# Half products of 64 rows beside attention's scores, in place of MLP and projection phases of their own

## The chip, the core and the metric

The kernel runs on one core of one Trainium2 chip. The metric is the device time of one execution in microseconds. Before the change it is 1593.18 us, the median of three runs (1592.98 to 1594.01).

## What is computed

One transformer block over 2,048 rows of 512 features, in fp32: layer norm, attention with 32 heads of 16 features over all rows, residual; then layer norm, an MLP with 1,792 hidden features, residual.

```python
qkv = (layernorm(x) @ wqkv).reshape(B, S, 3, 32, 16)
p = softmax(einsum("bhqd,bhkd->bhqk", q, k) * 16 ** -0.5)
h = x + einsum("bhqk,bhkd->bhqd", p, v).reshape(B, S, 512) @ wo
out = h + silu(layernorm(h) @ w1) @ w2
```

## The kernel before

**Number formats.** Projections and MLP are taken as three half-precision products each: a factor is split into a high and a low part of fp16, and high x high, low x high and high x low are summed. A "product" of one 128x512 tile of Q or K is 3 x 4 = 12 matmuls (`project_qk`, L590); a tile of the MLP's first layer is also 12; a tile of 128 output rows of its second layer is 3 x 14 = 42. Each of these matmuls contracts over 128 rows.

**Attention** is cut into 32 items: four blocks of 512 queries times eight sets of four heads. An item has 16 groups of 128 keys, 512 groups in all. A group (`scores`, L462; `values`, L856) is:
- four scores, one for each head: a matmul of 64 rows (48 rows of split Q and K and some with the row maximum, so that the product comes out with the maximum taken off), into a bank of PSUM; two heads of an item lie in rows 0 to 63 of TensorE's array, two in rows 64 to 127;
- an exponential on ScalarE for each score, from PSUM into a tile `pt`;
- four values, one for each head: `pt` as the moving fp32 operand, 17 columns of V and a column of ones as the stationary one, accumulated over the item's groups in the bank `pv`. They run two groups behind the scores (`LAG = 2`).

**Maxima.** The softmax's row maximum must be known before an item's scores. For each item 64 matmuls of 48 rows give Q K again, and VectorE reduces each bank to a maximum (`maximum`, L285: L301 reduces one bank, L299 two at once). A maximum of one row half stands beside a score of the other half. There are 2,048 of them, and they must be done one item ahead:

```python
            mm(space[:, n + m, :], qs[i % RING][64 * h:64 * h + 48, a, qt * P:qt * P + P],
               ks[i % RING][64 * h:64 * h + 48, a, kb * 512:kb * 512 + 512], start=True, stop=True)
        ...
            pin(nc.vector.tensor_reduce(of[:, j:j + 1], space[:, n, :], axis=AX.X, op=ALU.max))
```

A planner (`maxima`, L1324) says in each group how many maxima are issued, at most three. Finished maxima are turned and written into the rows of Q through DRAM or from PSUM (`place_far`, L338, `place_max`, L351).

**Order.** Every engine's queue follows the program text (`keep_in_program_order`), so the order is written out by hand. `soon` and `tick` delay steps by whole groups. The sequence is:
1. The projections of V and of the first set of Q and K, with maxima in pairs of banks (`burst`, L438) beside them.
2. 24 late projections, Q and K of the other three sets for four blocks, each with six maxima in pairs; the first two groups' scores stand between the last ones.
3. Attention, in which Q and K of coming items are loaded into a ring of five (`RING`).
4. In items 8, 16 and 24 (`FIRSTS`) the output projection of the block before (`output`, L1184), and after each of them that block's MLP (`finish_block`, L1204, `mlp`, L1118) with attention standing still: 14 first products with Silu, then the second layer in four accumulators, with 138, 138 and 110 maxima (`BESIDE`) in pairs between. The scores of the next two groups stand at its end.
5. After the last item the output projection and MLP of the last block (`finish_last`, L1221).

**PSUM** has eight banks of 128x512 fp32 (`space`). In attention scores take turns in four of them (`st`), maxima in three (`sm`), and one is `pv`:

```python
    attention_banks = 4, 5, last_bank, idle_bank
    lay_out(st=range(4), sm=attention_banks[:3])
    pv = space[:, idle_bank, :]
```

**Weights** of the MLP are split early in attention (`split_weights`, L1003, from group 12 on, one tile in four groups), stored to DRAM and read back tile by tile (`load_weights`, L989) into a ring of eight: w1 once and w2 twice for each block.

Of the kernel before, what the change touches and what calls it, by code (L numbers as in the profile page):

```python
# [43 lines left out]
SPLIT = 12  # L44
# [4 lines left out]
PTS = 16  # L49

EARLY = 8

RING = 5
# [12 lines left out]
JOINT = 2  # L66
AHEAD = 4
# [4 lines left out]
BESIDE = (138, 138, 110)  # L72
OUTPUT = 8

# [10 lines left out]
SPAN_2 = 12 * (FC - 2) - 3  # L85

MORE = 2, 2, 0
# [3 lines left out]
def attention_mlp_kernel(ctx: ExitStack, tc: tile.TileContext, x, wqkv, wo, w1, w2, out):  # L91
# [5 lines left out]
    def mm(*a, **k):  # L97
        tc.keep_in_program_order(nc.tensor.matmul(*a, **k))  # L98
# [12 lines left out]
    def act(fn, *a, **k):  # L111
        pin(getattr(nc.scalar, fn)(*a, **k))  # L112
# [80 lines left out]
    factors = const.tile([P, 14], F32, name="factors")  # L193
    sigma, inverse = factors[:, :4], factors[:, 4:8]
    w1_s, w2_s, wo_s, o_s = (sigma[:, n:n + 1] for n in range(4))
    h_f, g_s, out_f, wo_f, o_minus, o_twice = (factors[:, n:n + 1] for n in range(8, 14))
# [141 lines left out]
    def place_far(piece):  # L338

        i, _ = piece  # L340
        mt = small.tile([P, 32], F16, name="mt")
        dve("transpose", mt, split.pop(piece))
        issue = dma_beside if at["beside"] else dma
# [27 lines left out]
    at = {"item": 0, "done": 0, "half": 0, "step": 0, "due": 0, "attention": False, "group": None, "ready": 0, "next": 0, "blocks": True, "beside": False}  # L371
# [20 lines left out]

    def found_maxima(piece):
        g = at["group"]
        marked = g is not None and g + 1 in marks
        if g is None or marked or piece[1] is None and start_of(piece) - g > FAR:
            soon(WAIT + 1 if g is None or marked else CALM, place_far, piece)
            finish_max(piece, marked)
            return
        late.setdefault(at["step"] + WAIT, []).append(piece)  # L400
        unfinished.append(piece)
        found_at["step"] = at["step"]

    def one_max(half=None, n=None):
# [7 lines left out]
        if at["blocks"]:  # L412

            i = min(range(2), key=lambda n: (todo[n, half] or todo[n, 1 - half] or [(n, KC)])[0][1])
# [6 lines left out]
    def two_max(n):  # L421

        i = next_item()
        if i == ITEMS:
            return
        both = [next(((t[1], m, t) for t in todo[m, 0] if (*t[:4], 1) in todo[m, 1]), None)
                for m in (range(2) if at["blocks"] else (i,))]
        both = min((x for x in both if x), default=None)
# [26 lines left out]
    pts, den, pools = {}, {}, []  # L455
    taken = iter(range(10 ** 6))

    def pt_tile(name, dtype=F32):
        pool_of = pools[next(taken) % PTS >= EARLY]
        return pool_of.tile([P, 512], dtype, tag="pt", name=name)  # L460

    def scores(g, k, kind="st"):  # L462
# [7 lines left out]
        pts[g, k] = pt_tile("pt")  # L470
        act("activation", pts[g, k], ps, AF.Exp, scale=qk_f)


    with ExitStack() as pa:
        pb = pa.enter_context(ExitStack())
        lay_out(sm=range(5), st=range(5, 8))
        wp = pa.enter_context(tc.tile_pool(name="wp", bufs=1))
        wvp = pb.enter_context(tc.tile_pool(name="wvp", bufs=1, side="right"))
        xp = pa.enter_context(tc.tile_pool(name="xp", bufs=3))
        wqk_h = wp.tile([P, DC, 2 * D], F16, name="wqk_h")  # L480
        wqk_l = wp.tile([P, DC, 2 * D], F16, name="wqk_l")
        wv_h = wp.tile([P, DC, D], F16, name="wv_h")
        wv_l = wp.tile([P, DC, D], F16, name="wv_l")
        xth = [wp.tile([P, DC, 512], F16, name=f"xth{b}") for b in range(NB)]
        xtl = [wp.tile([P, DC, 512], F16, name=f"xtl{b}") for b in range(NB)]

        wqk0_h, wqk0_l = (wvp.tile([P, DC, 2 * P], F32R, name=name) for name in ("wqk0_h", "wqk0_l"))
        wv0_h, wv0_l, xth0, xtl0 = (wvp.tile([P, DC, 512], F32R, name=name) for name in ("wv0_h", "wv0_l", "xt0_h", "xt0_l"))

        xts = [ks[2 + b % 2].rearrange("p a n -> p (a n)").bitcast(F32).rearrange("p (t d) -> p t d", d=D)  # L490
               for b in range(NB)]

        scaled = ks[RING - 1].rearrange("p a n -> p (a n)").bitcast(F32).rearrange("p (t n) -> p t n", n=512)
        scaled, staged = ([scaled[:, t, :] for t in half] for half in ((0, 1), (2, 3)))
        flat = va.rearrange("p c h d -> p (c h d)")
        raw_v, *raw_qk = (flat[:, -n * DC * D:][:, :DC * D].rearrange("p (c n) -> p c n", c=DC) for n in (3, 2, 1))

        def load_x(b, parts=1):
            n = 4 // parts
            for t in range(0, 4, n):  # L500
                r0 = b * 512 + t * P
                dma(xts[b][:, t:t + n, :], x[r0:r0 + n * P, :].rearrange("(t p) d -> p t d", p=P))

        sq = small.tile([P, 3], F32, name="sq", bufs=1)

        free = qs[RING - 1].rearrange("p a n -> p (a n)").bitcast(F32)
        rest_sq, norms = free[:, :sum(PIECES)], free[:, 64:68]
        pieces = [w.rearrange("(p r) f -> p (r f)", p=P)[:, 512 * n:512 * (n + 1)]
                  for w, count in zip((w1, w2, wo), PIECES) for n in range(count)]

        def square_into(out, src, n):
            act("activation", out, src, AF.Square, accum_out=rest_sq[:, n:n + 1])

        def square_rest(u):

            n = u - 7
            if 0 <= n < len(pieces):
                square_into(staged[n % 2], staged[n % 2], n)
            n = u - 5
            if 0 <= n < len(pieces):  # L520
                dma_beside(staged[n % 2], pieces[n])

        def measure_rest():
            n = sum(PIECES)
            ps = bank("sm")
            mm(ps[:, :n], ones, rest_sq, start=True, stop=True)
            dve("tensor_reduce", norms[:, :2], ps[:, :28].rearrange("p (a k) -> p a k", a=2), axis=AX.X, op=ALU.add)
            dve("tensor_reduce", norms[:, 2:3], ps[:, 28:n], axis=AX.X, op=ALU.add)
            pool("tensor_scalar", norms, norms, 1e-30, None, op0=ALU.add)
            pool("tensor_tensor", norms, norms, expos, ALU.pow)  # L530

        def set_factors():
            dve("tensor_scalar", sigma[:, :3], norms[:, :3], TOP, None, op0=ALU.mult)
            dve("tensor_scalar", sigma[:, 3:], norms[:, 3:], TOP / BOUND, None, op0=ALU.mult)
            dve("tensor_scalar", sigma.bitcast(U32), sigma.bitcast(U32), 0x7F800000, None, op0=ALU.bitwise_and)
            dve("reciprocal", inverse, sigma)
            for to, a, f in ((h_f, inverse[:, :1], 1 / LN), (g_s, w1_s, 1 / 32.0), (o_minus, o_s, -1.0),
                             (o_twice, o_s, 2.0), (out_f, inverse[:, :1], 32.0)):
                pool("tensor_scalar", to, a, f, None, op0=ALU.mult)
            pool("tensor_tensor", out_f, out_f, inverse[:, 1:2], ALU.mult)  # L540
            pool("tensor_tensor", wo_f, inverse[:, 2:3], inverse[:, 3:], ALU.mult)

        def square(n, raw):
            act("activation", ks[RING - 1].rearrange("p a n -> p (a n)").bitcast(F32).rearrange(
                "p (c n) -> p c n", c=DC), raw, AF.Square, accum_out=sq[:, n:n + 1])

        def split_scaled(high, rest, raw, scale, engine="dve"):
            act("mul", high, raw, scale)
            if engine == "pool":
                pool("tensor_scalar", raw, raw, scale, 1.0, op0=ALU.mult, op1=ALU.mult)  # L550
                low(rest, raw, high, engine)
            else:
                dve("scalar_tensor_tensor", rest, raw, scale, high, op0=ALU.mult, op1=ALU.subtract)

        def split_qk(n, engine="dve"):
            g, key = divmod(n, 2)
            cols = slice(key * D + g * P, key * D + (g + 1) * P)
            split_scaled(wqk_h[:, :, cols], wqk_l[:, :, cols], raw_qk[key][:, :, g * P:(g + 1) * P], qk_w, engine)

        def split_first(key):  # L560
            cols, raw = slice(key * P, (key + 1) * P), raw_qk[key][:, :, :P]
            act("copy", wqk0_h[:, :, cols], raw)
# [887 lines left out]
```

## Time and profile before

| | |
|---|---|
| median of the runs | 1593.18 us |
| span of the profiled execution, first to last instruction | 1591.2 us |
| TensorE, VectorE, ScalarE, GpSimd busy | 99%, 87%, 76%, 30% of the span |
| late projections, 6th to 24th | 110.0 to 178.7 us |
| MLPs of blocks 0, 1 and 2 | 93.1, 93.0 and 87.6 us |
| after the last exponentials | 91.7 us |

The profile gives the span of its execution and no other time of it; the runs' median is 2.0 us longer than that span, and what lies around the span is taken as these 2.0 us. In the profile's rows PE is TensorE, DVE VectorE, ACT ScalarE, POOL GpSimd and SP SyncE, whose queue issues most DMAs. A row of the timeline has start and duration in us, engine, line, operation, and what is written from what; L98, L105, L112 and L115 are lines of helpers, so instructions are told apart by their tiles: `ps<-qs,ks` is a score, `ps<-ks,qs` a maximum's matmul, `ps<-pt,va` a value, `pt<-ps` an exponential, `mx<-ps` a reduce.

### The profile page before, as it was taken

How to read it: one execution, taken by the hardware profiler on the slowest of the kernel's cores; microseconds unless marked ns; L12 is line 12 of the kernel's file. 1: busy time of each engine (PE TensorE's matmuls, PEld its weight loads, DVE VectorE, ACT ScalarE, POOL GpSimd, SP SyncE). 2: the span in 40 equal slices, each digit the busy share in tenths (PEclk: the TensorE clock that was granted, in tenths of full speed). 3: DMA queues.
4: the chain of work that ended last, by engine and by line, in shares of the span. 5: the costliest groups of instructions: out<-in, count | busy, mean ns of one | idle time of the engine just before them, and what ended most of it. 6: DMA issues, size and time to landing. Idle time of an engine off the chain costs nothing. (4 is left out here: it accounts for less than half of the span.)

```text
span 1591.2 us, 28420 instructions
## 1 busy us (share of the span) xinstructions
PE 1579.5 (99%) x10476; PEld 471.7 (30%) x10476; DVE 1386.9 (87%) x2045; ACT 1205.0 (76%) x2384; POOL 484.8 (30%) x764
## 2 busy tenths in 40 slices
PE   9999999999999999999999999999999999999999
PEld 6434222222223322222224322222224322222254
DVE  7999999999998889999988889999986889998432
ACT  6545799999964179999973179999974189999732
POOL 5643544544446101211146101211146101211200
PEclk9999999999999999999999999999999999999999
DMA  6667533443443511121243521112143511100232
GB/s 216 174 177 221 136 86 91 113 119 86 116 100 102 157 47 35 38 51 44 50 102 101 152 53 34 39 41 53 48 104 108 159 40 37 34 12 22 74 87 73
DMA packets 124099, 140.29 MB, mean 88 GB/s; under 512 B 41808, under 2 KB 78736, under 8 KB 123960
## 3 DMA queue, kind: packets, MB, share of 16 engines
q1 hardware_dynamic: 117744, 128.34, 30.5%
q10 hardware_dynamic: 6216, 10.15, 2.3%
q8 instruction: 82, 1.34, 0.4%
q14 instruction: 57, 0.47, 0.1%
HBM read 104.68 MB, written 24.85 MB: 81 GB/s over the span
## 5 line engine op out<-in xcount | busy, mean ns | idle before, releaser
L112 ACT ACTIVATE pt<-ps 128x512 f32<-128x512 f32 x2048 | 1009.3, 611 | 154.4 <-PE ps L98 154.0
L301 DVE TENSOR_REDUCE mx<-ps 128x1 f32<-128x512 f32 x1470 | 925.1, 684 | 48.2 <-PE ps L98 20.3
L98 PE MATMUL ps<-pt,va 128*17 128x512 f32 x4096 | 537.5, 598 | 1.1
L98 PE MATMUL ps<-qs,ks 64*128 64x512 f16 x2048 | 530.9, 379 | 1.5 <-DMA qs<-mn 0.4
L98 PE MATMUL ps<-ks,qs 48*128 48x512 f16 x2048 | 495.4, 380 | 2.6 <-ACT pvs L112 1.1
L299 DVE TENSOR_REDUCE mx<-ps 128x2 f32<-128x1024 f32 x289 | 334.9, 1219 | 43.8 <-PE ps L98 42.5
L98 PEld LDWEIGHTS <-ks 64*128 64x128 f16 x2048 | 149.3, 95 | 549.2 <-issue 432.5
L105 POOL TENSOR_TENSOR ri<-rc,minus 128x16 f32<-128x16 f32 x31 | 90.7, 2926 | 242.5 <-DMA rc<-dn 192.3
L98 PE MATMUL ps<-w,gh 128*128 128x512 f16 (+1 forms) x678 | 154.4, 378 | 0.0
L98 PE MATMUL ps<-hts,w 128*128 128x512 f16 (+1 forms) x708 | 153.3, 369 | 0.0
L98 PEld LDWEIGHTS <-qs 48*128 48x128 f16 x2048 | 126.1, 94 | 77.5 <-issue 61.3
L98 PEld LDWEIGHTS ps<-pt,va 128*17 128x17 f32 x4096 | 69.0, 95 | 225.7 <-issue 205.4
L112 ACT ACTIVATE g<-ps,factors 128x512 f32<-128x512 f32 x56 | 38.4, 686 | 125.0 <-PE ps L98 95.7
L105 POOL TENSOR_TENSOR mx<-mx 128x32 f32<-128x32 f32 x52 | 12.6, 241 | 386.4 <-DVE mx L301 379.8
L98 PEld LDWEIGHTS <-w 128*128 128x128 f16 x708 | 66.5, 98 | 78.6 <-issue 10.2
L98 PEld LDWEIGHTS <-gh 128*128 128x128 f16 x678 | 63.1, 98 | 82.9 <-issue 13.7
L112 ACT ACTIVATE ks<-ps 128x512 f32<-128x512 f32 x30 | 17.9, 598 | 50.5 <-PE ps L98 45.1
L115 DVE SCALAR_TENSOR_TENSOR gh<-g,factors,gh 128x512 f16<-128x512 f32 x14 | 10.5, 751 | 52.1 <-ACT gh L112 52.1
L105 POOL TENSOR_TENSOR sl<-ks,sh 128x512 f16<-128x512 f32 x30 | 34.7, 1157 | 51.5 <-ACT sh L112 38.1
L105 POOL TENSOR_TENSOR gh<-g,gh 128x512 f16<-128x512 f32 x42 | 48.6, 1156 | 3.5
L105 POOL TENSOR_TENSOR ot<-ot,den 128x512 f32<-128x512 f32 (+1 forms) x16 | 20.4, 1273 | 84.4 <-DMA den<-dr 75.8
L98 PE MATMUL ps<-xth,wqk_h 128*128 128x512 f16 x120 | 45.8, 381 | 0.0
(155 smaller groups left out, 919.7 us busy)
## 6 DMA issues: line engine op xcount, KB each, us to landing
w<-w2d SPq DMA_DIRECT2D x98, 256.0 KB
ks<-kd SPq DMA_DIRECT2D x120, 192.0 KB
w<-w1d SPq DMA_DIRECT2D x56, 256.0 KB
ks<-in_B_w_dram ACTq DMA_DIRECT2D x28, 256.0 KB
w<-in_B_w_dram SPq DMA_DIRECT2D x28, 256.0 KB
qs<-qd SPq DMA_DIRECT2D x128, 48.0 KB
kd<-sh SPq DMA_DIRECT2D x16, 256.0 KB
qd<-sh SPq DMA_DIRECT2D x16, 256.0 KB
```

Of the source, the lines that this page charges most:

```text
L98: tc.keep_in_program_order(nc.tensor.matmul(*a, **k))
L105: tc.keep_in_program_order(getattr(nc.gpsimd, op)(*a, **k))
L112: pin(getattr(nc.scalar, fn)(*a, **k))
L115: pin(getattr(nc.vector, fn)(*a, **k))
L299: pin(nc.vector.tensor_reduce(of, space[:, n:n + 2, :], axis=AX.X, op=ALU.max))
L301: pin(nc.vector.tensor_reduce(of[:, j:j + 1], space[:, n, :], axis=AX.X, op=ALU.max))
```

## The change

The work of the late projections from the sixth on and of the MLPs of blocks 0 to 2 is put into attention's groups. A matmul over 128 rows becomes two over 64 rows: `half_product` gives rows 0 to 63 of it in an even group and rows 64 to 127 in the following odd one, both accumulated in one bank, number 3. For that the groups are taken in twos: in such a group the four scores are all of one row half, two of the group and two of its neighbour, and the half products stand in the other row half. `beside_products` lays the steps out: one list for the half products' side, one for the scores' side, maxima put where the lists are shorter.

- 5 late projections stay before attention, with six maxima in pairs each. 19 follow as "chains" of 12 products: five at six half products a group (four groups each), 14 at four (six groups each), so in groups 0 to 103.
- An MLP is 14 chains of 12 and four chains of 42 products at six half products a group, 112 groups after each output item. All results of the first layer are kept (`gates`), w2 is read four times, and Silu is computed as z/2 (1 + tanh(z/2)), with the tanh on ScalarE and the rest on GpSimd.
- In these 440 groups scores have three banks in place of four; maxima keep three; the planner gives four maxima, three where a finished maximum is being placed, and one more where it lags behind (`LEAD`). In the 72 other groups its most is four.
- A group's first half product waits for the last exponential of the group before (`fence`), so that half products of the two row halves don't write the bank at once. At the end of a chain the bank is scaled into SBUF by ScalarE ahead of the last exponential.
- Values run one group behind in these groups. The ring of items has four places. Squares of the weights for their scales, 14 of them, move into attention's first groups. Pool and tile memory is laid out anew.

The diff, cut to its core:

```diff
+SPLIT = 34
+SPACING = 3
-PTS = 16
+PTS = 12
-RING = 5
+RING = 4
-AHEAD = 4
+AHEAD = 6
-BESIDE = (138, 138, 110)
+LEAD = 9
+SWAP = 112
-BURSTS_1 = ({f: 6 for f in range(FC) if f not in (6, 13)},) * 2 + ({f: 6 for f in range(FC) if f % 3 != 1},)
-BURSTS_2 = 12, 12, 10
...
+    def after(ins, earlier):
+        tc.add_manual_dep(ins.ins, earlier.ins.name, mybir.DependencyInfo(
+            mybir.DependencyClass.Sync, mybir.DependencyReason.DATA), reason="row halves in one bank")
...
-        for g in range(1, NG // 2):
-            for m, (b, key) in enumerate([(b, 1) for b in range(NB)] + [(b, 0) for b in range(NB)]):
+    for m, (b, key) in enumerate([(b, 1) for b in range(NB)] + [(0, 0)]):
+        tick()
...
+        project_qk(b, 2 + key, {BESIDE_A1[m]: 6} if m < len(BESIDE_A1) else BESIDE_A, True)
...
-        elif i in FIRSTS:
+        elif i > FIRSTS[0]:
             act("copy", pvs, pv)
...
+    def end_first(f, ps):
+        z = zp.tile([P, 512], F32, name="g")
+        act("mul", z, ps, h_f)
+        def bend():
+            t = zp.tile([P, 512], F32, name="t", tag="oh")
+            act("activation", t, z, AF.Tanh, scale=0.5)
+            pool("tensor_scalar", t, t, 1.0, g_half, op0=ALU.add, op1=ALU.mult)
+            pool("tensor_tensor", t, t, z, ALU.mult)
+            pool("tensor_copy", gates[:, f, 0], t)
+            low(gates[:, f, 1], t, gates[:, f, 0], "pool")
+        soon(2, bend)
...
+    def begin_mlp(b):
+        chains.extend((3 * DC, 6, first_of(f), lambda ps, f=f: end_first(f, ps)) for f in range(FC))
+        chains.extend((3 * FC, 6, second_of(t), lambda ps, t=t: end_second(b, t, ps)) for t in range(4))
+
+    def half_product(j):
+        if j == 0:
+            current["open"].append(next(current["of"]))
+        lhs, rhs = current["open"][current["half"][j] - current["gone"]]
...
+        r = slice(64 * j, 64 * j + 64)
+        ins = mm(space[:, 3, :], lhs[r], rhs[r], start=current["half"] == [0, 0],
+                 stop=current["half"][1] == current["count"] - 1)
+        if "fence" in current:
+            after(ins, current.pop("fence"))
+        current["half"][j] += 1
+
+    def beside_products(g, n):
...
+        side = g % 2
+        heads = [(x, k) for x in (g - side, g - side + 1) for k in range(4) if head(x, k)[1] != side]
...
+        count = current["count"] - current["half"][0] if side == 0 else current["half"][0] - current["half"][1]
+        count = min(current["share"], count)
+        for _ in range(min(n, sum(left))):
+            j = 1 - side
+            if 4 + found[j] > count + found[side] or found[j] == left[j]:
+                j = side
+            if found[j] == left[j]:
+                j = 1 - j
+            found[j] += 1
+        other = [("max", 1 - side)] * found[1 - side]
+        other = [step for m, of in enumerate(heads) for step in [("score", of), *other[m:m + 1]]]
+        same = [("max", side)] * found[side] + [("half", side)] * count
+        short = len(same) - len(other)
+        if short > 0:
+            other[-1:-1] = [("none", 0)] * short
+        waiting = []
+        for m in range(max(len(other), len(same))):
+            for kind, x in same[m:m + 1] + other[m:m + 1]:
+                if kind == "score":
+                    waiting.append(scores(*x))
+                    if len(waiting) < 4:
+                        waiting[-1]()
+                elif kind == "max":
+                    one_max(x)
+                elif kind == "half":
+                    half_product(x)
+        if current["half"][1] == current["count"]:
+            current["end"](space[:, 3, :])
+            current.clear()
+            waiting[3]()
+        else:
+            current["fence"] = waiting[3]()
...
+    first_qk = [(b, 5) for b in range(NB)] + [(0, 4)]
+    other_qk = [(b, 7) for b in range(NB)] + [(0, 6)] + [(b, n) for n in (2, 4, 6) for b in range(1, NB)]
+    chains.extend((3 * DC, share, rows_of_qk(b, n), lambda ps, b=b, n=n: end_qk(b, n, ps))
+                  for units, share in ((first_qk, 6), (other_qk, 4)) for b, n in units)
+    until = 4 * len(first_qk) + 6 * len(other_qk)
+    beside = {*range(until), *(g for m in marks for g in range(m, m + 4 * FC + 4 * FC))}
...
     def maxima(g):
+        ready = at["ready"] = min(ITEMS, i + RING - 1) * 64
+        most = 3 if at["step"] in late else 4
+        if g in beside:
+            at["due"] = 0
+            most += 64 + 4 * (g + LEAD) > at["done"]
+            return max(0, min(most, ready - at["done"]))
...
-        most = 2 if at["step"] in late or c == JOINT and i and i - 1 not in FIRSTS else 3
...
         if g in marks:
-            finish_block(i // 8 - 1, (g - 2, g - 1))
+            begin_mlp(i // 8 - 1)
+            lay_out(st=range(3))
+        elif g - 1 in beside and g not in beside:
+            lay_out(st=range(4))
...
-        if g - LAG >= 0 and not (g in marks or g - 1 in marks):
-            values(g - LAG)
+        while done <= g - (1 if g in beside else LAG):
+            values(done)
+            done += 1
```

Here `scores` returns a function that issues the exponential, so that the last one of a group can be issued behind the chain's end.

More of the change, by code (lines that the diff above doesn't have):

```diff
@@ L342, in place_far @@
         dve("transpose", mt, split.pop(piece))
-        issue = dma_beside if at["beside"] else dma
+        issue = dma
         for b in range(4):
@@ L370, in attention_mlp_kernel @@
     END = 64 * ITEMS
-    at = {"item": 0, "done": 0, "half": 0, "step": 0, "due": 0, "attention": False, "group": None, "ready": 0, "next": 0, "blocks": True, "beside": False}
+    at = {"item": 0, "done": 0, "half": 0, "step": 0, "due": 0, "attention": False, "group": None, "ready": 0, "next": 0, "blocks": True, "loaded": 1}
     agenda, late = {}, {}
@@ new lines, in split_values, with project_v @@
+    def split_values(n):
+        half = slice(2 * n, 2 * n + 2)
+        act("mul", wv_h[:, half], raw_v[:, half], v_w)
+        if n:
+            low(wv_l[:, 2], scaled[1], wv_h[:, 2], "pool")
+        else:
+            low(wv_l[:, 3], scaled[0], wv_h[:, 3], "pool")
+            dve("scalar_tensor_tensor", wv_l[:, half], raw_v[:, half], v_w, wv_h[:, half],
+                op0=ALU.mult, op1=ALU.subtract)
+    def project_v(b, t):
+        ps = bank()
+        weave(product(ps, lambda c: xth[b][:, c, t * P:(t + 1) * P], lambda c: xtl[b][:, c, t * P:(t + 1) * P],
+                      lambda c: wv_h[:, c, :], lambda c: wv_l[:, c, :], DC),
+              {k: (lambda n=n: burst(n)) for k, n in BESIDE_V1.get((b, t), {}).items()})
+        act("mul", va[:, 4 * b + t, :, 0:DH], ps.rearrange("p (h d) -> p h d", d=DH), v_f)
@@ new lines, in turn_x, with columns @@
+    def turn_x(b, t):
+        turn(xts[b][:, t, :], xth[b][:, :, t * P:(t + 1) * P], xtl[b][:, :, t * P:(t + 1) * P],
+             "sm" if b == 1 else "st")
+    load_x(0, parts=4)
+    for dc in range(DC):
+        dma(raw_v[:, dc, :], wqkv[dc * P:(dc + 1) * P, 2 * D:])
+    for key in (1, 0):
+        for dc in range(DC):
+            dma(raw_qk[key][:, dc, :], wqkv[dc * P:(dc + 1) * P, key * D:(key + 1) * D])
+    load_x(1, parts=4)
+    def columns(t):
+        return slice(t * P, (t + 1) * P)
@@ new lines, in idle, with turn_high @@
+    def idle(n):
+        ps = bank()
+        for c in range(n):
+            tr(ps[:, columns(c % 4)], ident, ident)
+    def turn_high(b, t):
+        ps = bank("sm").rearrange("p (c n) -> p c n", n=P)
+        high = xth[b] if b else xth0
+        for c in range(4):
+            tr(ps[:, c, :], xts[b][:, t, c * P:(c + 1) * P], ident)
+        act("copy", high[:, :, columns(t)], ps)
+        return ps
+    idle(20)
+    found = [statistics(xts[0][:, t, :], LN) for t in range(2)]
+    turned, ps_vs = [], []
@@ new lines, in first_rows, with first_products @@
+    def first_rows(t):
+        normalize(xts[0][:, t, :], xts[0][:, t, :], *found[t])
+        turned.append(turn_high(0, t))
+    def first_products(t, *chunks):
+        if t == len(ps_vs):
+            ps_vs.append(bank("st" if t < 3 else "sm"))
+        for c in chunks:
+            mm(ps_vs[t], xth0[:, c, columns(t)], wv0_h[:, c, :], start=c == 0, stop=False)
+    first_rows(0)
+    idle(4)
+    found.append(statistics(xts[0][:, 2, :], LN))
+    act("copy", wv0_h[:, 0, :], raw_v[:, 0, :])
@@ L1051, in split_normal @@
     def split_normal(t):
-        rows, halves[t] = hx.pop(t), parts_of(gp.tile([P, 512], F32, name="g"))
+        rows, halves[t] = hx.pop(t), parts_of(zp.tile([P, 512], F32, name="g"))
         act("copy", halves[t][:, 0], rows)
@@ L1202, in output @@
             found[n] = statistics(rows_of(b, n), LN)
-    def finish_block(b, pending):
-        act("activation", small.tile([P, 1], F32, name="sw"), ident[:, :1], AF.Silu)
-        load_weights("w1", 4)
-        for g in pending:
-            values(g)
-        mlp(b)
     O = ot[(NB - 1) % 2]
```

864 lines of the change are left out of this document (407 added, 457 removed).

## The prediction

> **What bounds the kernel now.** I read the page's engine shares and slices first, then one table of windows cut at the stages, then the timeline of single groups.
>
> ```profile
> PE 1579.5 (99%) x10476; PEld 471.7 (30%) x10476; DVE 1386.9 (87%) x2045; ACT 1205.0 (76%) x2384; POOL 484.8 (30%) x764
> ACT  6545799999964179999973179999974189999732
> ```
>
> TensorE shows 99%, but a busy TensorE is not one at its peak, so this alone says little. ScalarE says what the change is about: it is full in attention and nearly empty three times between, in the MLPs.
>
> ```profile
> 110.00:178.70 68.70, 68.70 (x356) 27.00 (x354) 68.03 (x74) 36.32 (x75) 28.55 (x40) 1.00 0.63 190
> 178.70:427.30 248.60, 247.80 (x1883) 55.24 (x1883) 236.96 (x385) 248.17 (x506) 123.54 (x185) 1.00 0.41 108
> 427.30:472.10 44.80, 44.48 (x295) 11.58 (x295) 41.31 (x70) 34.46 (x70) 16.68 (x24) 1.00 0.41 87
> 472.10:565.20 93.10, 92.38 (x476) 35.84 (x468) 82.46 (x79) 23.69 (x35) 35.94 (x59) 1.00 0.44 123
> 786.60:831.80 45.20, 44.68 (x295) 11.59 (x295) 41.37 (x70) 34.52 (x71) 16.70 (x24) 1.00 0.34 76
> 831.80:924.80 93.00, 92.35 (x476) 35.83 (x468) 82.69 (x79) 23.63 (x34) 34.48 (x53) 1.00 0.44 123
> 1146.30:1189.50 43.20, 43.00 (x289) 11.53 (x289) 37.73 (x64) 34.53 (x71) 16.70 (x24) 1.00 0.36 79
> 1189.50:1277.10 87.60, 87.24 (x448) 34.36 (x440) 66.31 (x63) 23.58 (x34) 33.84 (x50) 1.00 0.44 130
> 1499.50:1591.20 91.70, 88.15 (x466) 44.09 (x456) 27.74 (x48) 24.61 (x38) 3.17 (x8) 1.00 0.25 69
> ```
>
> Columns: stretch, length, then busy time of PE, weight loads, DVE, ACT, POOL, granted clock, DMA share, GB/s. The rows are the 19 late projections (68.7 us), attention up to the first output item, each output item with its MLP, and the tail. In the MLPs ACT is busy 24 of 93 us, but DVE 82 of 93, because the maxima go on there in pairs. So the idle engine is ACT alone; DVE and TensorE have little left to fill. The clock is 1.00 throughout.
>
> Now one attention group on TensorE:
>
> ```profile
> 255.42 0.39 PE L98 MATMUL ps<-qs,ks 64*128 64x512 f16 x1
> 255.42 0.60 PE L98 MATMUL ps<-ks,qs 48*128 48x512 f16 x2
> 255.65 0.59 PE L98 MATMUL ps<-qs,ks 64*128 64x512 f16 x2
> 255.87 0.38 PE L98 MATMUL ps<-ks,qs 48*128 48x512 f16 x1
> 256.08 0.38 PE L98 MATMUL ps<-qs,ks 64*128 64x512 f16 x1
> 256.39 1.05 PE L98 MATMUL ps<-pt,va 128*17 128x512 f32 x8
> 257.38 0.39 PE L98 MATMUL ps<-qs,ks 64*128 64x512 f16 x1
> ```
>
> A score of one row half and a maximum of the other start together; such a step takes (256.08 - 255.42) / 3 = 0.22 us. From the last step to the values is 0.31, from there to the next group 0.99. A group is 3 x 0.22 + 0.31 + 0.99 = 1.96 us with three maxima. Its fixed part is 1.30.
>
> ```profile
> 243.66 0.60 PE L98 MATMUL ps<-ks,qs 48*128 48x512 f16 x2
> 244.12 1.89 DVE L301 TENSOR_REDUCE mx<-ps 128x1 f32<-128x512 f32 x3 [0.30 <-PE ps L98]
> L301 DVE TENSOR_REDUCE mx<-ps x290: 679/681/693, 235.5 to 429.9; 128x1 f32<-128x512 f32 x145
> 1345.26 0.69 DVE pvs L115
> 1345.95 0.04 issue
> 1345.99 60.91 PE ps L98 x464
> 564.80 0.61 PE L98 MATMUL ps<-qs,ks 64*128 64x512 f16 x4
> 565.22 2.06 ACT L112 ACTIVATE pt<-ps 128x512 f32<-128x512 f32 x4 [40.56 <-PE ps L98]
> L112 ACT ACTIVATE pt<-ps x395: 591/603/646, 235.7 to 429.8; 128x512 f32<-128x512 f32 x198
> ```
>
> DVE waits for nothing else when its reduce starts 244.12 - 243.66 = 0.46 after the maximum's matmul; a reduce takes 0.68 and they follow at (1.89 - 0.68) / 2 = 0.60. TensorE starts 0.04 after the DVE ends (the chain of waits, last three rows of it). So a bank of a maximum is free again 0.46 + 0.68 + 0.04 = 1.18 us after its matmul started. An exponential starts 0.42 after its score, follows the one before at (2.06 - 0.60) / 3 = 0.48, and takes 0.60. Three maxima use 1.80 of 1.96 on DVE, four exponentials 1.92 on ACT: all three engines are near balance in attention, with TensorE the longest.
>
> **The change, part by part.** Durations are of the profiled execution; the median is 1593.2 and the span 1591.2, so 2.0 goes on top.
>
> *What ends earlier.* The fifth late projection ends where it does now, so attention begins at 110 instead of 178.7.
>
> ```profile
> 106.50 0.60 ACT L112 ACTIVATE ks<-ps 128x512 f32<-128x512 f32 x1 [1.74 <-PE ps L98]
> 110.11 0.60 ACT L112 ACTIVATE ks<-ps 128x512 f32<-128x512 f32 x1 [1.74 <-PE ps L98]
> 109.42 0.38 PE L98 MATMUL ps<-xth,wqk_l 128*128 128x512 f16 x1
> 109.64 0.38 PE L98 MATMUL ps<-xtl,wqk_h 128*128 128x512 f16 x1
> 109.85 0.38 PE L98 MATMUL ps<-xth,wqk_h 128*128 128x512 f16 x1
> ```
>
> The second row is that unit's evacuation, 3.61 after the one before; TensorE begins the sixth unit at 109.85. From 110 to the end of attention are 1499.5 - 110 = 1389.5 us now; 68.7 of projections and 93.1 + 93.0 + 87.6 = 273.7 of MLP go out of it, and 440 groups get work beside them.
>
> *What a half product costs.* The trace has none. Below: a full product of 128 rows starts every 0.215 (the last rows), and a half fills only half the array, so it could be free beside a score; above: it takes a step of its own half, 0.22, as the maximum does. I take a step, the nearest row, since K is 64 against 48. Two halves beside each other or beside a score then cost what the full product did: the 1,236 moved products save nothing on TensorE by themselves. (The Trainium skill, TensorEngine Tiling, Instruction Overhead, gives each matmul about 60 cycles of overhead; at 512 columns per 0.215 us that is an estimated 0.025 us, and 1,236 more matmuls would add 31 us to the sum. The rows above, 512 columns every 0.215 back to back, leave no room for it, so I add nothing.)
>
> *Maxima.* Before attention there are 74 (`BESIDE_V` and `BESIDE_V1`) + 5 x 6 = 104, where now there are 216, and none are left in an MLP of their own. So 1,944 single reduces lie in attention, 3.8 a group where there were about 3, and 1,944 x 0.60 = 1,166 us of DVE. Stepping the planner's rule group by group: four in each of the first 104; in the 72 plain groups 43 times four and 29 times three or two; in the 336 MLP groups 42 times five, 25 times none at the end, else about four.
>
> *The new wait.* The maxima have three banks. In a plain group today they sit at steps 0, 1, 2 and never wait. A fourth must wait for the first one's bank, until 1.18, and on the in-order TensorE queue the scores, half products and values behind it wait too; ScalarE waits for those scores.
> - Late projections (share 4): the split puts two maxima on each side, at steps 0, 1, 1 and 3. TensorE alone would need 5 x 0.22 + 1.30 = 2.40. The fourth goes from 0.66 to 1.18, two score steps follow: 1.18 + 0.44 + 1.30 = 2.92.
> - Share 6, four maxima: one and three, at steps 0, 1, 3, 5. TensorE alone 6 x 0.22 + 1.30 = 2.62; the fourth moves from 1.10 to 1.18: 2.70.
> - Five maxima: the fifth needs the second one's bank, 0.46 + 0.60 + 0.68 + 0.04 = 1.78, then the values: 3.08.
> - Plain group, four maxima: 1.18 + 1.30 = 2.48, else 1.96.
>
> *The fence.* The first half product of a group waits for the last exponential of the one before. With a last score at 1.40: it starts at 1.40 + 0.42 or behind the others at 0.42 + 3 x 0.48 = 1.86, ends 2.46, free 2.50; the half product stands at step 1 of the next group, 2.92. Hidden, with 0.42 to spare. In the 25 groups without maxima it stands first, and the group is 2.50 instead of 2.40.
>
> *ScalarE and POOL.* The scaling and the tanh add two ACT operations in four groups. Neither form is in the trace; bounds are an exponential (0.48) and the gate's scaling, 0.72:
>
> ```profile
> L112 ACT ACTIVATE gh<-g,factors 128x512 f16<-128x512 f32 x56 | 40.4, 722 | 1.8
> L105 POOL TENSOR_TENSOR gh<-g,gh 128x512 f16<-128x512 f32 x42 | 48.6, 1156 | 3.5
> L112 ACT ACT_TABLE_LOAD x8 | 10.3, 1283 | 0.8 <-PEq L1436 0.7
> ```
>
> Four groups of 2.70 leave ACT 4 x 0.78 = 3.1 us; covered. POOL's four operations, at most 1.16 each, have four groups of 2.70. The Silu tables that go were loaded while ACT idled: nothing.
>
> *DMA.* w2 is read four times a block instead of twice: one 256 KB tile per group of 2.70, 97 GB/s, against 190 GB/s moved in the first window above. Five tiles ahead on SP's queue: hidden.
>
> *MLP start.* The first half product waits for the transposed rows.
>
> ```profile
> 469.67 2.97 SPq L125 DMA_TRANSPOSE hts<-g  x2
> 471.00 2.77 PE L98 MATMUL ps<-pt,va 128*17 128x512 f32 x24
> 475.18 3.19 PE L98 MATMUL ps<-hts,w 128*128 128x512 f16 x14
> ```
>
> Today two groups of pending values and six maxima bridge up to 475.18; the new group would be there about 472.2. Between 0 and 3.0 a block; I take 2.0.
>
> *Sum.* 20 x 2.70 = 54.0; 84 x 2.92 = 245.3; 269 x 2.70 = 726.3; 42 x 3.08 = 129.4; 25 x 2.50 = 62.5; 43 x 2.48 = 106.6; 29 x 1.96 = 56.8; the output products beyond 31.4 an item, 13.4 + 13.8 + 11.8 = 39.0; 6.0 at MLP starts. Together 1425.9 against 1389.5: +36.4. The tail has one pending group of values less, -1.0. 1591.2 + 35.4 + 2.0 = **1628.6**, say 1628. Against groups of 1.96 the late projections lose 27, the MLPs win 8 and the plain groups lose 22; today's groups are 5 longer in all than 1.96 each, which leaves the 36.
>
> **The rivals.**
> 1. *No bank wait* (faster). If TensorE lets the steps of the other row half pass a waiting maximum, or the maxima fall so that a bank is always free, groups go at TensorE's 2.62 and 2.40, five maxima at DVE's 5 x 0.60 = 3.00, four in a plain group at 2.40: 52.4 + 201.6 + 704.8 + 126.0 + 62.5 + 103.2 + 56.8 + 45.0 = 1352.4, so -37.1 - 1.0: 1555. It decides below a mean of 2.68 over the 440 groups ((1217.5 - 35.4 - 3.2) / 440; the forecast's is 1217.5 / 440 = 2.77). For it: no group in the trace waits so. Against: the three banks, and the rows' 1.18.
> 2. *ScalarE late* (slower still). If scaling, tanh or copies push the last exponential by over 0.42, the fence ends last. Some 96 groups hold such an operation; 0.35 each is 34 us: 1662. Against: 0.78 spare a group.
> 3. *Table switches*. If tanh needs another table than exp, 42 groups get two loads of 1.28, less the 0.78 spare: 42 x 1.8 = 75 us, 1703. The trace has only Silu's eight loads. (The Trainium skill, ScalarE: Activation LUTs, Table sets, puts exp and tanh in one set; by it no load is added. No run so far shows it.)
> 4. *Halves that don't overlap*: some three more steps in 440 groups, 0.66 each: +290 us, 1918. Against: the scores and maxima that start together above.
>
> **How the numbers follow.** Forecast 0.60, rival 1 0.20, rival 2 0.08, rivals 3 and 4 0.03 together; 0.09 for a bank wait about half as long, 1590 to 1610. A difference under 0.2% (3.2 us) is about what a measurement of this kernel can't tell from none. Faster 0.22 (rival 1 and a little of the half wait), same 0.05, slower 0.73. The forecast's own range is 1605 to 1650 (a step of 0.216 to 0.23, MLP starts of 0 to 3). Out to rivals 1 and 2 it is 1580 to 1660, which leaves out the lower part of rival 1 (0.12) and the upper cases (0.07).
>
> **What would show it.** Right: attention begins at about 110; late-projection groups repeat every 2.9 and MLP groups every 2.7; the fourth maximum's matmul starts 0.04 after the DVE ends the first; DVE idles some 0.3 a group in the MLPs and 0.5 in the late projections; ACT is no longer full. Wrong: groups of 2.4 and 2.6 with DVE full (rival 1); more than two table loads (3); half products that start 0.22 apart from their scores instead of with them (4); first half products that follow the exponential at 0.04 (2).

## The result, and the profile after

The changed kernel takes 1655.44 us (median of four runs, 1655.2 to 1656.14) against 1593.16 us before: 1.039 times as long, 95% interval 1.0375 to 1.0404. 62 us slower; 35 were forecast. 1655 lies above the forecast's own range of 1605 to 1650, and inside the wide one of 1580 to 1660. The profiled execution has a span of 1654.4 us, 63.2 more than before.

The page of the changed kernel, shares and slices as shown for the one before:

```profile
PE 1603.7 (97%) x11711; PEld 475.3 (29%) x11711; DVE 1378.4 (83%) x2251; ACT 1250.5 (76%) x2403; POOL 579.6 (35%) x875
DVE  7989888888997999999997999999988999992232
ACT  5549878787885788887876888878776788888632
```

ScalarE's three gaps are gone, but its share stands at 76% as before: it is no longer full in attention either. Nothing was gained by filling it. DVE's busy time is nearly the same in a longer span: its share falls from 87% to 83%, TensorE's from 99% to 97%.

The stages, in the same table of windows (length, busy time of PE, weight loads, DVE, ACT, POOL, granted clock, DMA share, GB/s): groups 0 to 103 with the late projections, groups 104 to 143 with the first output item, then MLP groups, a stretch of 16 plain ones with an output item, and so on up to the tail.

```profile
113.50:421.10 307.60, 289.31 (x2113) 71.07 (x2110) 264.97 (x437) 249.18 (x481) 122.48 (x190) 0.98 0.36 103
421.10:530.50 109.40, 102.04 (x668) 22.85 (x667) 101.04 (x171) 85.27 (x169) 46.75 (x70) 1.00 0.37 97
530.50:842.10 311.60, 308.62 (x2484) 86.19 (x2486) 285.08 (x465) 252.41 (x488) 101.44 (x154) 0.99 0.34 90
842.10:891.50 49.40, 46.43 (x288) 11.74 (x284) 43.42 (x75) 35.92 (x72) 20.46 (x36) 1.00 0.35 88
891.50:1202.60 311.10, 308.12 (x2482) 86.00 (x2484) 283.55 (x463) 252.84 (x488) 101.32 (x154) 0.99 0.34 90
1202.60:1250.20 47.60, 44.92 (x286) 11.77 (x280) 40.27 (x70) 35.64 (x71) 18.91 (x30) 1.00 0.36 90
1250.20:1562.10 311.90, 307.19 (x2396) 85.81 (x2398) 233.95 (x390) 252.09 (x487) 97.74 (x137) 0.99 0.31 87
```

An MLP with its 112 groups is 311 us. Before it was 93 of MLP and 112 x 1.96 = 220 of groups, 313 (307 for the third): the MLP's own stage bought next to nothing, and the late projections and the plain groups lost. Counted between the first exponentials of the same groups in both traces, the changed kernel loses 41.5 us from 110 us to group 104 and 23.2 in the plain stretches, and wins 2.1 in the three MLPs.

Where the time goes shows in one late-projection group of the changed kernel's timeline (start, duration, engine, line, tiles; `ps<-qs,ks` a score, `ps<-ks,qs` a maximum's matmul, the rows with `wqk` half products):

```profile
301.27 0.39 PE L98 MATMUL ps<-ks,qs 48*128 48x512 f16 x1
301.27 0.39 PE L98 MATMUL ps<-qs,ks 64*128 64x512 f16 x1
301.50 0.38 PE L98 MATMUL ps<-ks,qs 48*128 48x512 f16 x2
301.69 2.49 DVE L308 TENSOR_REDUCE mx<-ps 128x1 f32<-128x512 f32 x4 [0.40 <-PE ps L98]
301.71 0.38 PE L98 MATMUL ps<-xth,wqk_h 64*128 64x512 f16 x1
301.72 0.38 PE L98 MATMUL ps<-qs,ks 64*128 64x512 f16 x1
301.94 0.37 PE L98 MATMUL ps<-xth,wqk_l 64*128 64x512 f16 x1
302.44 0.37 PE L98 MATMUL ps<-ks,qs 48*128 48x512 f16 x1
302.45 0.39 PE L98 MATMUL ps<-xtl,wqk_h 64*128 64x512 f16 x1
302.66 0.38 PE L98 MATMUL ps<-qs,ks 64*128 64x512 f16 x1
302.67 0.38 PE L98 MATMUL ps<-xth,wqk_h 64*128 64x512 f16 x1
302.88 0.37 PE L98 MATMUL ps<-qs,ks 64*128 64x512 f16 x1
303.07 1.08 ACT L112 ACTIVATE pt<-ps 128x512 f32<-128x512 f32 x2 [0.25 <-PE ps L98]
303.18 1.05 PE L98 MATMUL ps<-pt,va 128*17 128x512 f32 x8
304.16 0.39 PE L98 MATMUL ps<-ks,qs 48*128 48x512 f16 x1
```

The half product at 301.94 should be followed by the fourth maximum at about 302.16 at the latest; it starts at 302.44, 1.17 after the first maximum of the group (301.27). Two scores and the values stand behind it, and both ScalarE (idle 0.25 at 303.07) and DVE (idle 0.40 at 301.69) run out of work. The group is 304.16 - 301.27 = 2.89 us. The matmul that waits is one that DVE holds up, though DVE itself idles in each such group.

### The profile page after: what moved, and what is told of

The parts are those of the page before. It is cut to its first block, busy times and chain, and to the rows that moved or that the text cites. A ratio compares the mean times of both kernels' runs of the same rounds, so it can differ in the third digit from the quotient of the medians.

```text
span 1654.4 us, 31785 instructions
## 1 busy us (share of the span) xinstructions
PE 1603.7 (97%) x11711; PEld 475.3 (29%) x11711; DVE 1378.4 (83%) x2251; ACT 1250.5 (76%) x2403; POOL 579.6 (35%) x875
## 4 chain that ended last, share of the span: by engine, by line
PE 75%; DVE 14%; ACT 4%; DMA 2%; POOL 2%; issue 2%; SPq 1%; POOLq 0%; ACTq 0%; DVEq 0%
PE ps L98 75%; DVE mx L308 10%; ACT pt L112 3%; DVE mx L306 1%; SPq L128 1%; DMA hts<-g 1%; DVE st L122 1%; PE ps L101 0%; POOL ri L105 0%; ACT t L112 0%; DMA va<-in_A_wqkv_dram 0%; DMA ks<-in_A_x_dram 0%; DVE pvs L122 0%; POOL oh L105 0%; DMA rc<-dn 0%
## 5 line engine op out<-in xcount | busy, mean ns | idle before, releaser
L308 DVE TENSOR_REDUCE mx<-ps 128x1 f32<-128x512 f32 x1944 | 1206.3, 683 | 115.5 <-PE ps L98 113.5
L98 PE MATMUL ps<-qs,ks 64*128 64x512 f16 x2048 | 723.8, 380 | 3.8 <-ACT pt L112 1.8
L98 PE MATMUL ps<-ks,qs 48*128 48x512 f16 x2048 | 641.6, 380 | 31.2 <-DVE mx L308 15.5
L98 PE MATMUL ps<-hts,w 64*128 64x512 f16 (+2 forms) x1212 | 287.8, 373 | 7.0 <-DMA hts<-g 7.0
L98 PE MATMUL ps<-w,gates 64*128 64x512 f16 x1008 | 245.0, 376 | 1.3
L98 PEld LDWEIGHTS <-w 64*128 64x128 f16 (+1 forms) x1212 | 114.0, 95 | 139.0 <-issue 43.7
L98 PEld LDWEIGHTS <-gates 64*128 64x128 f16 x1008 | 92.6, 94 | 128.1 <-issue 28.0
L98 PE MATMUL ps<-xth,wqk_h 64*128 64x512 f16 (+1 forms) x196 | 75.1, 383 | 0.3 <-ACT pt L112 0.3
L98 PE MATMUL ps<-xth,wqk_l 64*128 64x512 f16 (+1 forms) x196 | 75.1, 383 | 0.0
L306 DVE TENSOR_REDUCE mx<-ps 128x2 f32<-128x1024 f32 x52 | 60.1, 1219 | 3.7 <-PE ps L98 3.5
```

The lines of the kernel that those rows point to most:

```text
L98: return tc.keep_in_program_order(nc.tensor.matmul(*a, **k))
L306: pin(nc.vector.tensor_reduce(of, space[:, n:n + 2, :], axis=AX.X, op=ALU.max))
```

## The experiments

**The order inside the late groups.** Both own-side maxima stood at the head of the list; here the second goes to its end.

```diff
         same = [("max", side)] * found[side] + [("half", side)] * count
+        if count == 4 and found[side] > 1:
+            same.append(same.pop(0))
```

> Only the order inside the 84 groups with four half products changes: the second maximum of the half products' side is issued last instead of at step 1, so the maxima stand at steps 0, 1, 3 and 5. The same instructions, the same engine loads. Theory (the fourth maximum waits for the first one's bank, and scores and values wait behind it): these groups go from 2.89 to 5 x 0.22 + 0.08 + 1.30 = 2.48 us, 84 x 0.41 = 34 us less, 1621. Rival A (VectorE's throughput sets the groups): the load is the same, no change, 1655. Rival B (the half products take more of TensorE than a step): no change, 1655.

Measured 1626.81 us, 28.6 less. The same group type in its timeline:

```profile
250.16 0.39 PE L98 MATMUL ps<-ks,qs 48*128 48x512 f16 x1
250.39 0.38 PE L98 MATMUL ps<-ks,qs 48*128 48x512 f16 x1
...
250.83 0.38 PE L98 MATMUL ps<-ks,qs 48*128 48x512 f16 x1
...
251.33 0.37 PE L98 MATMUL ps<-ks,qs 48*128 48x512 f16 x1
251.34 0.39 PE L98 MATMUL ps<-qs,ks 64*128 64x512 f16 x1
251.66 1.05 PE L98 MATMUL ps<-pt,va 128*17 128x512 f32 x8
252.64 0.39 PE L98 MATMUL ps<-ks,qs 48*128 48x512 f16 x1
```

The fourth maximum again starts 1.17 after the first, but now it stands in the last step, where it would have come at 1.10 anyway, and nothing is behind it but the values. This group, an even one, is 2.48 (252.64 - 250.16). Not one instruction is removed, so neither DVE's throughput nor the half products' own cost set the 2.89: the place of the waiting instruction in the queue does.

The odd groups are 2.56, 0.08 more than the theory has. Their values read exponentials of the same group; in the one from 258.10 to 260.66 the second exponential ends at 259.64, and the value that needs it starts at 259.70, 0.09 after the three before it. The eight value matmuls then take 1.14 in place of 1.05:

```profile
258.56 2.07 ACT L112 ACTIVATE pt<-ps 128x512 f32<-128x512 f32 x4
259.59 1.14 PE L98 MATMUL ps<-pt,va 128*17 128x512 f32 x8
```

In the profiled executions the 84 groups are 28.4 shorter, where 34 were expected. The start took 0.8 more there and the first MLP's start 1.6 less; the last section shows why that start can differ.

**Six half products in the late chains too.**

```diff
-                  for units, share in ((first_qk, 6), (other_qk, 4)) for b, n in units)
-    until = 4 * len(first_qk) + 6 * len(other_qk)
+                  for units, share in ((first_qk, 6), (other_qk, 6)) for b, n in units)
+    until = 4 * len(first_qk) + 4 * len(other_qk)
```

> The 14 late chains that take four half products a group take six: 56 groups in place of 84, and 28 groups become plain ones. Theory (bank wait): 84 x 2.89 = 243 us become 56 x 2.68 + 28 x about 2.33 = 215, so 27 us less, 1628. Rival A (VectorE's throughput): the same maxima in the same number of groups, 1655. Rival B (TensorE's steps): the same half products, within 5 us of 1655.

Measured 1632.47 us, 23.0 less. The late groups then repeat every 2.67 to 2.68, and the 28 groups set free are plain ones, most of them of 2.49; their mean is 2.40, where 2.33 was expected. With more half products in a group the fourth maximum comes later by itself and waits less. Both rivals said no change, or hardly any.

**Shorter reduces.** Each reduce in attention reads half of its bank; half of every maximum is left out.

```diff
-            pin(nc.vector.tensor_reduce(of[:, j:j + 1], space[:, n, :], axis=AX.X, op=ALU.max))
+            pin(nc.vector.tensor_reduce(of[:, j:j + 1], space[:, n, :256], axis=AX.X, op=ALU.max))
```

> In attention each reduce reads 256 of the 512 columns, so half of every maximum is left out; TensorE's and ScalarE's work stay. A bank of a maximum is then held about 0.3 us shorter, 0.9 in place of 1.18, and VectorE's load in attention falls by some 45%. Theory: four maxima at steps 0, 1, 1, 3 wait till about 0.9 (2.63), the others not at all: MLP groups 2.62, plain ones 1.96. 84 x 0.26 + 269 x 0.055 + 42 x 0.21 + 43 x 0.5 = 67 us less, 1588. Rival A (throughput): about the same, since VectorE is far from full then, but with the late groups at TensorE's 2.40, 1570. Rival B (TensorE's steps): 1655.

Measured 1599.24 us, 56 less. The groups of reduces, in the changed kernel and here (count, busy time, mean ns of one, DVE's idle time before them):

```profile
L308 DVE TENSOR_REDUCE mx<-ps 128x1 f32<-128x512 f32 x1944 | 1206.3, 683 | 115.5 <-PE ps L98 113.5
```

```profile
L308 DVE TENSOR_REDUCE mx<-ps 128x1 f32<-128x256 f32 x1944 | 729.8, 420 | 510.2 <-PE ps L98 507.2
```

DVE loses 476 us of work and the kernel 56 of time. The group types went to a median of 2.62 (late), 2.61 (MLP), 2.83 (five maxima) and 2.22 (plain with four). The late ones keep 0.22 over TensorE's 2.40, because the bank is still held 0.46 + 0.42 + 0.04 = 0.92 there; so the theory's 2.63, not the throughput rival's 2.40. The plain ones with four were put at 1.96 and kept 0.26 for the same reason, and the trace has 34 of them besides the output items: 34 x 0.26 = 9 of the 11 us by which the sum was missed. Both types stay above TensorE's time while DVE idles, so it is the bank and not DVE's throughput that holds them.

**MLPs alone in the groups.** All late projections ahead of attention as before, each with six maxima, items 2 and 3 loaded beside them.

```diff
-    for m, (b, key) in enumerate([(b, 1) for b in range(NB)] + [(0, 0)]):
+    for g in range(1, NG // 2):
+        for m, (b, key) in enumerate([(b, 1) for b in range(NB)] + [(b, 0) for b in range(NB)]):
...
-    until = 4 * len(first_qk) + 6 * len(other_qk)
+    until = 0
...
-        ready = at["ready"] = min(ITEMS, i + RING - 1) * 64
+        ready = at["ready"] = min(ITEMS, i + RING - 1 + (i == 0)) * 64
```

> All 24 late projections stand ahead of attention again, with six maxima in pairs each; only the MLPs stay in attention's groups. Theory: groups 0 to 103 (308 us with the late chains) become 69 us of projections and 104 plain groups of about 1.98, 206; with 108 maxima more done ahead the other plain groups hold three instead of four, 22 us less, and the slow start, 7 us, goes: 62 us less, 1593. Rival (the MLPs in the groups are the loss, the late projections not): at most 20 us less, 1635 or more.

Measured 1659.56 us: the expectation missed by 67. The rival's number (1635 or more) came out, but not for the rival's reason. The windows of the maxima's operations over groups 0 to 15, 16 to 31 and 32 to 111 (DVE, POOL, clock, DMA):

```profile
177.70:214.30 36.60, 24.41 (x39) 1.24 (x5) 0.95 0.17 47
214.30:253.80 39.50, 0.00 (x0) 0.00 (x0) 0.96 0.27 67
253.80:443.20 189.40, 179.26 (x289) 4.98 (x20) 1.00 0.38 103
```

The maxima done ahead were lost at once: with a ring of four, item 4 can't be loaded before item 0 is through, so DVE did no maximum in groups 16 to 31. From group 32 on the planner needed 289 / 80 = 3.6 a group, and a plain group with four maxima costs 2.49. I had put these groups at 1.98. So this run doesn't separate the two parts of the change. It does show that a fourth maximum makes a group without any half product longer too (2.49 against 1.96), and that here the maxima ahead were worth nothing beyond the ring.

**The factors earlier.** The call is moved ahead of the five late projections.

```diff
     at["blocks"] = False
+    set_output_factors()
...
-    set_output_factors()
     pb.close()
```

> The factors of the attention output are computed ahead of the five late projections instead of behind them. Theory (at attention's start VectorE's queue stands behind these factors, which wait for GpSimd, which waits for a DMA, and TensorE goes to half clock meanwhile): groups 0 and 1 take 2.7 us each instead of 6.2 and 4.4, 5 us less, 1650. Rival (the rows of the maxima that land late set the start): less than 1 us, 1655.

Measured 1652.12 us, 3.3 less, but the four runs spread from 1649.95 to 1655.56, and the profiled one is the slowest. In it groups 0 and 1 took 3.05 and 3.01 in place of 6.21 and 4.43, 4.6 less, as expected. In the runs that leave the start alone and keep the late chains beside attention, the two took 9.9 to 11.8 together, so this is no chance. But the third MLP's first group took 9.36 in place of 8.11, because TensorE's clock stayed at half for 6.83 us there in place of 3.41, and two more stretches at half clock stand elsewhere: the whole gain in the times of the groups is 0.6 in that execution. So the cause is shown, and its worth only roughly. The first score still stood 0.83 for the rows with the maxima.

**Two MLPs two groups later.**

```diff
-    marks = [KC * (8 * b + 1) for b in range(1, NB)]
+    marks = [KC * (8 * b + 1) + (2 if b < NB - 1 else 0) for b in range(1, NB)]
```

> The MLPs of blocks 0 and 1 begin two groups later in attention, the third as before; the two groups are plain ones. Theory (the first half product waits for the transposed rows, TensorE idles 2 us and then runs at half clock): the first two groups of these MLPs go from 7.5 + 3.4 to 3.05 each, about 5 us for each of two, 1645. Rival (the cost is that of the first weights or of the queue, and moves along): 1655.

Measured 1643.5 us, 11.9 less. The first two groups of the first MLP took 4.45 and 3.12, in place of 7.54 and 3.44, of the second 3.66 and 3.12. The wait didn't move along; it was the transposed rows. The expected 3.05 for the first group wasn't reached, since two groups' values stand in it (16 value matmuls in place of 8). Counted up to the same later group, with the two plain groups in, the starts give 4.5 and 5.5 us, the 10 expected. The other 2 us were not expected; they come mostly from first groups of items, before which a chain no longer ends: six of them take 2.83 in place of 3.37.

**The three together.** The edits of the order, of the factors and of the later MLPs.

> The order with the second own maximum last, the early factors and the later MLPs together. Theory: the three are separate, 28.6 + 5 + 10 us less: 1612, still slower than before, because VectorE and TensorE have no room for the moved work. Rival (they share the same slack): 1620 or more.

Measured 1612.52 us, 42.9 less: the three add up (28.6 + 3.3 + 11.9 = 43.8). It is 1.0119 times the kernel before (1.0103 to 1.0136).

**The three and shorter reduces.** Half of every maximum is left out again.

> As the last one, and each reduce in attention reads 256 of the 512 columns, so half of every maximum is left out. Theory (what is left against the kernel before is the banks that the maxima hold): the late groups reach TensorE's 2.40, 84 x 0.2 = 17 us less than with short reduces alone, and 15 us from the two starts: 1567, faster than before. Rival (TensorE's steps alone already cost more than the phases saved): 1590 or more.

Measured 1570.04 us, 0.9859 (0.9842 to 0.9875) of the kernel before, and 29 less than with shorter reduces alone, where 32 were expected. Only the even late groups come near TensorE's 2.40 (2.39 or 2.44); the odd ones stay at 2.56, with the values' wait described above. With the three edits and halved reduces the changed kernel stands 23 us below the kernel before, with the three edits alone 19 above it. That the difference is the banks' alone is not shown, since the halved reduces also take work off DVE; and the kernel before was not run with halved reduces, so the 23 us are not what moving the work is worth by itself. No version that computes everything beat the kernel before.

## Why the prediction was right

**The group times.** Each type's median in the changed kernel against its sum, from the starts of every fourth exponential:

| group | forecast | measured |
|---|---|---|
| late, four half products, four maxima | 2.92 | 2.89 |
| six half products, four maxima | 2.70 | 2.67 |
| five maxima | 3.08 | 3.05 |
| plain, four maxima | 2.48 | 2.49 |
| six half products, no maxima | 2.50 | 2.62 |

In the first four rows the 1.18 of a bank, the step of 0.22 for a half product and the 1.30 of values and switches hold to about 1%. An MLP group shows that a half product takes the other half's step and no more:

```profile
721.20 0.37 PE L98 MATMUL ps<-w,gates 64*128 64x512 f16 x1
721.20 0.38 PE L98 MATMUL ps<-qs,ks 64*128 64x512 f16 x1
721.41 0.37 PE L98 MATMUL ps<-w,gates 64*128 64x512 f16 x1
721.42 0.38 PE L98 MATMUL ps<-ks,qs 48*128 48x512 f16 x1
```

Half products start every 0.215, beside a score or a maximum. That settles rival 4. (The Trainium skill, TensorEngine Tiling (Array Packing), Instruction Overhead, gives each matmul about 60 cycles of overhead. In this trace a half product takes no more than the 0.215 of a full one, so the 31 us that the prediction names beside its sum are not there.)

**The rivals.** Rival 1, no bank wait, is out: the order alone was worth 28.6 us. The run nearest to its 1555, with halved reduces and the starts mended, is 1570. Rival 2's 1662 is nearer to the result than the forecast's 1628, but by number only: in no group with maxima does the first half product follow the last exponential by less than 0.10, while in those without, where the fence does bind, it is 0.06. Rival 3 is settled by ScalarE's groups of instructions in the changed kernel:

```profile
L112 ACT ACT_TABLE_LOAD x2 | 2.6, 1283 | 0.7 <-PEq L1521 0.7
L112 ACT ACTIVATE t<-g 128x512 f32<-128x512 f32 x42 | 27.2, 648 | 0.0
```

Two loads are left of eight, one at 0.7 us, which the kernel before has too, and one at 1564.3 us for the tail's Silu. The 42 tanhs run among the exponentials without one. So exp and tanh share a table here, as the Trainium skill (ScalarE: Activation LUTs, Table sets) has it.

**Where the sum was short.** The span is 1654.4 against 1626.6 forecast, 27.8 more. The medians of the groups with maxima lie some 11 us in all under their terms, so about 39 us more than the sum had lie elsewhere. The sum's terms for the edges are the steps that failed: the start at nothing, the MLPs' starts at 6 us.
- *Attention's start*, put at 109.85 with no cost. The first score starts at 112.85, 3.0 later, and groups 0 and 1 take 5.3 more than two usual ones: 8 us. This is the step "attention begins at 110": I moved the start past SP's and GpSimd's queues without counting what stood in them.

```profile
112.85 0.58 PE L98 MATMUL ps<-qs,ks 64*128 64x512 f16 x1 [0.80 <-DMA qs<-md]
114.80 1.15 POOL L105 TENSOR_TENSOR sl<-scaled,sh 128x512 f16<-128x512 f32 x1 [4.94 <-DMA kd<-sl]
116.04 0.23 POOL L105 TENSOR_SCALAR norms<-norms 128x1 f32<-128x1 f32 x1
116.96 0.15 DVE L122 TENSOR_SCALAR factors<-norms 128x1 f32<-128x1 f32 x1 [5.33 <-POOL norms L105]
117.42 2.46 DVE L308 TENSOR_REDUCE mx<-ps 128x1 f32<-128x512 f32 x4
118.15 0.58 PE L98 MATMUL ps<-ks,qs 48*128 48x512 f16 x1 [2.98 <-DVE mx L308]
```

  A chain over four engines: a DMA holds GpSimd's subtraction, this holds the factors' power on GpSimd, this holds a DVE instruction of 0.15 us, and behind that wait the first reduces and then TensorE. The run with the factors earlier takes out 4.6 of it.
- *MLP starts*, put at 2 each: the first two groups of the three MLPs are together 4.9, 4.6 and 5.0 over two usual ones, 8.5 in all over the forecast.

```profile
530.02 0.39 PE L98 MATMUL ps<-qs,ks 64*128 64x512 f16 x1
532.49 0.58 PE L98 MATMUL ps<-hts,w 64*128 64x512 f16 x1 [2.08 <-DMA hts<-g]
532.88 0.63 PE L98 MATMUL ps<-hts,w 64*128 64x512 f16 x1
```

  The wait itself is 2.08, what I took. Behind it TensorE runs at half clock for 3.41 us (matmuls of 0.63 every 0.4), which costs about half of that, 1.7. And two groups' values stand in the first group (2.04 in place of 1.05 in the first MLP), 1.0 more.
- *The 25 groups without maxima*, bound by the fence: the first exponential starts 0.49 after its score in them instead of 0.42, so most take 2.62 in place of 2.50: 3 to 4 us.
- The remainder, 18 to 19 us, is spread. Some 13 are single groups over their type's median, most of them near the first group of an item: in the MLPs 2.83 there in place of 2.67, or 3.37 where a chain has just ended; in the late projections 3.2 there, and two of 4.52. The output items take 2.5 more, and the tail 1.0, since it didn't get shorter. The few us left were not traced.

So the mechanism and the group types were right, and the size was low: of the 62 us the sum had 35. The attention's start was priced at nothing and the MLPs' starts by their wait alone, 17 us together, and the groups at items' edges were taken for usual ones.

## What to carry to other kernels

An engine that idles in a stage is worth filling only if the work that goes there doesn't need the engines that are full: here only ScalarE had gaps, and TensorE and VectorE were nearly full in both stages. When a step is added to a group, work out for each ring of buffers when the one it needs comes free, and look at what stands behind it in the in-order queue; a reorder without any saving was worth 28.6 us. And price a stage's edge by the wait, by the instructions queued in front of it on every engine, and by the clock after it.

## What the runs showed of the hardware

The granted clock falls after a short idle, but not after each one. Windows around the start of the first MLP in the changed kernel, and in the run with the reordered late groups (clock in the third column from the end), with the first half product of the latter:

```profile
529.08:532.49 3.41, 1.33 (x11) 0.21 (x11) 1.92 (x4) 1.99 (x4) 0.00 (x0) 1.00 0.66 144
532.49:535.90 3.41, 3.41 (x17) 1.11 (x21) 2.28 (x4) 1.79 (x3) 0.00 (x0) 0.50 0.50 145
```

```profile
504.96 0.37 PE L98 MATMUL ps<-hts,w 64*128 64x512 f16 x1 [2.08 <-DMA hts<-g]
500.21:503.62 3.41, 2.66 (x20) 0.53 (x16) 3.25 (x6) 2.59 (x5) 0.00 (x0) 1.00 0.45 86
503.62:507.03 3.41, 2.07 (x18) 0.84 (x22) 1.63 (x3) 1.43 (x3) 0.00 (x0) 1.00 0.91 237
```

In the changed kernel TensorE was idle for 2.08 us (530.41 to 532.49), and then ran at half clock for 3.41. In the other run it was idle for the same 2.08 at the same place of the program, and the clock stayed at 1.00: the MLP's first group took 5.95 in place of 7.54. So the same wait can cost 1.6 us more or less.

What differs is where the idle lies. In each of the ten traces all changes of the granted clock lie whole multiples of 3.41 us apart. Cut into such stretches, the changed kernel's idle lies in one of them whole, and the other run's is divided: TensorE was idle for 0.75 of the first and 1.34 of the second. Over the ten traces, from 20 us on, no stretch at full clock with 1.73 us of idle or more was followed by another at full clock; those that were had 1.66 at most. 28 of the 31 falls follow a stretch with 1.73 to 2.75 of idle; three, with 0.44, 1.38 and 1.50, don't fit. That TensorE's idle is weighed by stretches of 3.41 is an inference from this; no run here was made to test it. (The Trainium skill, TensorE: Matmul & The Clock Gate, Part 1, has the gate fall to half after an idle window of about 3.4 us. The length agrees with the 3.41 here, but in these traces about half of it idle was enough.)
